# Second operations of GpSimd's minima one step later, and 97 joint minima instead of 81, in a fused top-k attention and squared-ReLU FFN kernel

## The chip, the cores and the metric

The kernel runs on one core of a Trainium2 chip. The metric is device time in microseconds (us) of one execution, taken as the median of several runs. The engines are named as in the profile: PE (TensorE, with PEld for its weight loads), DVE (VectorE), ACT (ScalarE), POOL (GpSimd) and SP (SyncE, which here only issues DMAs).

## The reference

```python
B, H, S, D = 8, 8, 576, 64; top_k = 32
scores = matmul(q, k^T) / sqrt(D)                  # per batch and head, 576 x 576
kth    = the 32nd largest of each row
attn   = softmax over the entries >= kth, 0 elsewhere
x      = (attn @ v), heads side by side            # 4608 tokens x 512
out    = relu(x @ w_in)**2 @ w_out                 # 512 -> 2048 -> 512, float32
```

## The kernel before, in words

The attention is cut into 144 **steps**, numbered u = 0 to 143 (`U = 144`). A step takes two tiles of 128 query rows (index x = 0, 1), each against all 576 keys of its head. The FFN of finished tokens is cut into pieces that are put between the steps. One Python loop writes the instructions of all engines in program order (`pin` keeps that order on each engine); each engine runs its own queue in order and waits on semaphores for the others. A main loop writes steps 0 to 124 (`Z = 125`), a second one steps 125 to 141, and the last two are written out. `DEEP = 9`: after step 11 the preparation of a step runs two steps ahead (`lead = 2`). Step 66 begins near 400 us in the profile of before, step 122 near 720 us.

For each step, the 32nd largest of 576 scores is found by DVE in four rounds of "8 largest, then remove them" (`topk`: MAX8 on L282, MATCH_REPLACE8 on L286). The rounds do not look at all 576 scores: the scores are first sorted partly, so that large ones stand in front.

- `scores(u)`: PE multiplies into the two PSUM banks sc_a and sc_b (L202); ACT copies both to `s` (L207), sc_b first.
- `split(u)`, the **pairing**: scores 0 to 287 meet scores 288 to 575. DVE takes the maxima, `tops` (L235, 128x576 for both tiles). The matching **half minima** go to `cat[288:576]`. In a "lent" step POOL makes all of them; in a step that is not lent DVE makes a quarter itself, in three operations of half the size (L237, L238, L240).
- `bring(u)`: PE copies the second half of `tops` into a part of bank sc_b (`far`, L223), so that DVE can pair it with the first half.
- `join(u)`, the **join**: DVE pairs the two halves of `tops`: maxima to `cat[0:144]` (L250), minima to `cat[144:288]` (a second L250). In a **joint** step DVE makes only the maxima, and POOL the **joint minima**.
- POOL has no minimum in use here; it computes min(a, b) as a + b - max(a, b) on the numbers' bits as integers, in two operations: an addition into its place in `cat`, and a subtraction in place. `joint_mins` does so with 128x288 (L256, L257), `small_mins` for the half minima with 128x576, or 128x288 in a step not lent (L263, L264).

Round 0 of `topk` reads `cat[0:100]`, round 1 `cat[24:144]`, round 2 `cat[0:256]` (it needs the joint minima) and round 3 all (it needs the half minima). DVE's order within step u of the main loop is: `split(u+2)`, rounds 0 to 3 of u, `join(u+2)`. POOL's order is: both operations of the joint minima of u+1, both of the half minima of u+2, squares of the FFN, the mask of u-1 (L333), now and then a cast of v (L154). SP then issues the transpose DMA of the masked weights.

Who does what is set by a planner while the program is written. `debt["G"]` and `debt["A"]` are running estimates of what POOL and ACT still owe, in us: `owe` adds, and `pass_step` takes 5.8 (POOL) and 6.0 (ACT) off at each step. By these numbers a step is lent or not (`split`), joint or not (`join`), a square of the FFN goes to ACT (L517) or POOL (L520), and a weight cast to ACT (L607) or POOL (L604).

Of the kernel before, what the change touches and what calls it, by code (L numbers as in the profile page):

```python
# [15 lines left out]
i32 = mybir.dt.int32  # L16
ALU = mybir.AluOpType
# [5 lines left out]
def kernel(  # L23
# [9 lines left out]
    nc = tc.nc  # L33
# [10 lines left out]
    HALF, QUAR = S // 2, S // 4  # L44

    def pin(ins):
        tc.keep_in_program_order(ins)
        return ins

    debt = {"G": 0.0, "A": 0.0}  # L50

    def owe(**more):
        for e, t in more.items():
            debt[e] += t
# [2 lines left out]

    def pass_step(more=0.0):
        for e in debt:
            debt[e] = max(0.0, debt[e] - {"G": 5.8, "A": 6.0}[e] - more)  # L60

    const = ctx.enter_context(tc.tile_pool(name="const", bufs=1))
    fast = ctx.enter_context(ExitStack())
# [120 lines left out]
    U = len(steps)  # L184
    Z, DEEP = U - 19, 9
# [6 lines left out]
    st = {}  # L192
# [32 lines left out]
    def split(u):  # L225
        d = st[u]
        lend = (2 < u < U - 20 and debt["G"] < 4.9) or Z < u < U - 5
        cat = d["cat"] = scp.tile([128, 2, S], f32, name="cat", bufs=3)
        tops = d["tops"] = scp.tile([128, 2, HALF], f32, name="tops", bufs=3)
        one, two = sc[0][:, :, 0:HALF], d["s"][:, :, HALF:S]  # L230
        tt = nc.vector.tensor_tensor
        if lend:
            owe(G=1.22)
            d["lent"] = True
            pin(tt(tops[:, :, :], one, two, op=ALU.max))  # L235
        else:
            pin(tt(far, one[:, :, QUAR:HALF], two[:, :, QUAR:HALF], op=ALU.max))  # L237
            pin(tt(tops[:, :, 0:QUAR], one[:, :, 0:QUAR], two[:, :, 0:QUAR], op=ALU.max))  # L238
        if not lend:
            pin(tt(cat[:, :, HALF + QUAR:S], one[:, :, QUAR:HALF], two[:, :, QUAR:HALF], op=ALU.min))  # L240
        if "rest" in d:
            d.pop("rest")()

    def join(u):
        d = st[u]
        d["joint"] = "lent" in d and DEEP + 4 <= u < U - 6 and debt["G"] < (4.5 if u < Z + 2 else 5.5)
        if d["joint"]:
            owe(G=1.6)
        for lo, op in ((0, ALU.max), (QUAR, ALU.min))[0:1 if d["joint"] else 2]:
            pin(nc.vector.tensor_tensor(d["cat"][:, :, lo:lo + QUAR], far, d["tops"][:, :, 0:QUAR], op=op))  # L250

    def joint_mins(u):
        d = st[u]
        if d["joint"]:
            at, tops = d["cat"][:, :, QUAR:HALF].bitcast(i32), d["tops"][:, :, :].bitcast(i32)
            pin(nc.gpsimd.tensor_tensor(at, tops[:, :, 0:QUAR], tops[:, :, QUAR:HALF], op=ALU.add))  # L256
            pin(nc.gpsimd.tensor_tensor(at, at, d["cat"][:, :, 0:QUAR].bitcast(i32), op=ALU.subtract))  # L257

    def small_mins(u):
        d = st[u]  # L260
        n = HALF if "lent" in d else QUAR
        s, at = d["s"], d["cat"][:, :, HALF:HALF + n].bitcast(i32)
        pin(nc.gpsimd.tensor_tensor(at, s[:, :, 0:n].bitcast(i32), s[:, :, HALF:HALF + n].bitcast(i32), op=ALU.add))  # L263
        pin(nc.gpsimd.tensor_tensor(at, at, d["tops"][:, :, 0:n].bitcast(i32), op=ALU.subtract))  # L264

    GROUP = 18
    WINDOWS = (slice(0, 100), slice(24, QUAR), slice(0, 256), slice(0, S))
# [4 lines left out]
    def topk(u, rounds=(0, 1, 2, 3), between=None):  # L272
        d = st[u]
        g = u % GROUP
        if g == 0 and 0 in rounds:
            held_m["m"] = small.tile([128, GROUP, 2, 4, 8], f32, name="m", bufs=2)
        m = d["m"] = [held_m["m"][:, g, :, r, :] for r in range(4)]
        cat = d["cat"]
        for r in rounds:
            at = WINDOWS[r]  # L280
            for x in range(2):
                pin(nc.vector.max(out=m[r][:, x, :], in_=cat[:, x, at]))  # L282
            if r == 3:
                break
            for x in range(2):
                pin(nc.vector.match_replace(out=cat[:, x, at], in_to_replace=m[r][:, x, :], in_values=cat[:, x, at], imm_value=NEG))  # L286
            if r == 1:
                negate(u)
            if r == 2 and between:
                between()  # L290
        if g == GROUP - 1 and 3 in rounds and u < U - 1:
            verify(u)
# [353 lines left out]
    scores(0)  # L646
    split(0)
    join(0)
    small_mins(0)
    scores(1)  # L650


# [20 lines left out]
    for u in range(Z):  # L673
        now[0] = u
        f = u - 4
        lead = 2 if u > DEEP + 2 else 1
        pass_step()
        owe(A=4.5 if u < DEEP + 15 else 4.12, G=3.0)
        if u > 0:
            below(u - 1, 0)  # L680
        if u == 0:
            topk(0, (0, 1))
            split(1)
            join(1)
            topk(0, (2, 3))
        elif not DEEP < u < DEEP + 3:
            split(u + lead)
        if not DEEP < u < DEEP + 3:
            ahead(u + 1 + lead)
        if u > 0:  # L690
            topk(u, (0,))
        if u == DEEP + 2:
            join(u + 1)
            split(u + 2)
            ahead(u + 3)
            bring(u + 2)
        if ok(f) and f % 2:
            invert_two(f)
        if ok(f - 1):
            place(f - 1)  # L700
        if checks:
            note()
        if lead > 1:
            joint_mins(u + 1)
        if u == DEEP + 2:
            small_mins(u + 2)
        elif u != DEEP + 1:
            small_mins(u + lead)
        dense(u, 0)
        if u and not DEEP < u < DEEP + 3:  # L710
            bring(u + lead)
        if u > 0:
            below(u - 1, 1)
            topk(u, (1,))
            if u == DEEP + 1:
                join(u + 1)
            topk(u, (2,))
            if u == DEEP + 1:
                split(u + 2)
                small_mins(u + 2)  # L720
                ahead(u + 3)
                bring(u + 2)
            topk(u, (3,))
            if u == DEEP:
                join(u + 1)
                split(u + 2)
            elif u != DEEP + 1:
                join(u + 2 if u > DEEP else u + 1)
            exps(u - 1)
            mask(u - 1)  # L730
            turn(u - 1)
        flush()
        if u == Z - 1:
            assert u % 2 == 0
            products(u - 3)
            piece()
            expo(u, 0)
            expo(u, 1)
            piece()
        else:  # L740
            dense(u, 1)
            flush()
            products(u - 3)
        if u == DEEP:
            small_mins(u + 2)
            ahead(u + 3)
            bring(u + 2)
        for _ in range(2 if u < 8 or u in (U - 22, U - 19) else 1):
            prepare(u)
        if 1 < u < 24 and not ups and not downs:  # L750
            idle_piece(2)
        turn_x(u)
        if w_casts and u >= 4:
            w_casts.pop(0)()
        if w_loads and u >= 1:
            w_loads.pop(0)()

    def weights(w):
        mask(w)
        turn(w)  # L760
# [5 lines left out]
    for u in range(Z, U - 2):  # L766
        now[0] = u
        pass_step(0.3)
        owe(A=4.12, G=3.0)
        below(u - 1, 0)  # L770
        below(u - 1, 1)
        move()
        split(u + 2)
        topk(u, (0,))
        if u == Z:
            products(u - 3)
            invert_two(u - 4)
            place(u - 5)
            place(u - 4)
        if checks:  # L780
            note()
        joint_mins(u + 1)
        small_mins(u + 2)
        if u == U - 8:
            sums_checked(nc.gpsimd, 0, OLD)
        weights(u - 1)
        square()
        hold["squares"] = False
        for go in ripe.pop(u, ()):
            go()  # L790
        ahead(u + 3)
        topk(u, (1,))
        if not piece():
            idle_piece()
        bring(u + 2)
        products(u - 2)
        topk(u, (2, 3))
        join(u + 2)
        if u == Z:
            invert(u - 3)  # L800
        invert(u - 2)
        expo(u, 0)
        expo(u, 1)
        flush()
        if u == Z:
            place(u - 3)
        place(u - 2)
        turn_x(u)
        hold["squares"] = True
        for _ in range(2 if u == U - 19 else 1):  # L810
            prepare(u)
        for n in range(3 if u >= U - 12 else 2):
            if not piece() and n == 0:
                idle_piece()
# [10 lines left out]
    u = U - 2  # L825
# [5 lines left out]
    below(u - 1, 0)  # L831
    below(u - 1, 1)
    topk(u, (0,))
    weights(u - 1)
    while downs:
        piece()
# [15 lines left out]
    for x in range(2):  # L852
        below(u, x)
        at = w[:, x, 0:S].bitcast(i32)
# [44 lines left out]
    u = U - 1  # L899
# [185 lines left out]
```

## Time and profile before

| | |
|---|---|
| median of 3 runs | 873.14 us (872.8 to 873.77) |
| the profiled execution | 873.56 us, its span 871.6 us |
| TensorE clock granted | 0.988 of full speed |
| HBM traffic | 36.70 MB read, 9.44 MB written |
| DVE's operations that the change touches | L250 x207, L235 x131, L237, L238 and L240 x13 each |
| POOL's operations that the change touches | L256 and L257 x81 each, L263 and L264 x144 each, L520 x45 |

The span is from the first to the last instruction; some 2 us lie around it. In a row of a group, "xN" is the count, then come busy us and mean ns of one, then the engine's idle time ahead of them and what ended it. In a row of the timeline come the start (us from the span's start) and the duration; "xN" merges neighbours, and a bracket tells idle time and its releaser. A row of waits reads: engine, instruction, what it waited for, total us, times, longest.

### The profile page before, as it was taken

Reading aid. Unit: us, or ns where it says so; the run is one execution under the profiler, and the core shown is the slowest. Engines: PE = TensorE matmul, PEld = TensorE weight load, DVE = VectorE, ACT = ScalarE, POOL = GpSimd, SP = SyncE. Lnnn points to the kernel's source line nnn. Section 1 sums busy time; section 2 is a strip of 40 time slices with the busy share of each in tenths; the row PEclk is TensorE's granted clock in tenths of the full one; section 3 lists DMA queues with packets and bytes.
Section 4 is the critical chain, followed back from the end, with each engine's and each line's share of the span. In section 5 each row is a group of like instructions: output and inputs, shape, how many; then the busy total and the mean of one; then the engine's idle time right before and its main releaser. Section 6 shows DMA issues by size and latency. Waiting matters only on the chain.

```text
span 871.6 us, 19893 instructions
## 1 busy us (share of the span) xinstructions
PE 755.6 (87%) x5948; PEld 482.7 (55%) x6030; DVE 842.1 (97%) x3445; ACT 809.8 (93%) x1630; POOL 787.0 (90%) x722
## 2 busy tenths in 40 slices
PE   6998997888888988889889888889888898999986
PEld 3554555555555554555555555555655564666644
DVE  5999999999999999999999999999999999999994
ACT  2888999899999998999999999999999999999973
POOL 3688999999999999999999999999999998999752
PEclk7999999999999999999999999999999999999999
DMA  5597776546565566456565455655555655424352
GB/s 122 120 223 162 178 180 106 108 97 113 92 126 108 113 112 126 80 107 115 111 115 93 101 118 108 120 120 115 121 107 116 111 101 124 85 59 86 71 85 44
DMA packets 325442, 98.04 MB, mean 112 GB/s; under 512 B 317520, under 2 KB 317776, under 8 KB 325328
## 3 DMA queue, kind: packets, MB, share of 16 engines
q1 hardware_dynamic: 323984, 96.28, 56.0%
q8 instruction: 49, 0.80, 0.4%
q10 hardware_dynamic: 1344, 0.43, 0.2%
q14 instruction: 65, 0.53, 0.2%
HBM read 36.70 MB, written 9.44 MB: 53 GB/s over the span
## 4 chain that ended last, share of the span: by engine, by line
DVE 68%; PE 12%; issue 9%; ACT 7%; POOL 3%; DMA 1%; SPq 0%; ACTq 0%; DVEq 0%; POOLq 0%
DVE m L282 28%; DVE cat L286 20%; DVE tops L235 8%; DVE cat L250 7%; PE dn_ps L534 2%; PE gen L506 2%; PE sc_b L223 2%; ACT s L207 2%; PE sc_b L202 2%; PE av_ps L404 1%; PE sc_a L202 1%; POOL cat L263 1%; ACT marks_a L328 1%; ACT h L517 1%; ACT rl L512 1%
## 5 line engine op out<-in xcount | busy, mean ns | idle before, releaser
L282 DVE MAX8 m<-cat 128x8 f32<-128x100 f32 (+3 forms) x1152 | 435.3, 419 | 0.0
L286 DVE MATCH_REPLACE8 cat<-m,cat 128x100 f32<-128x100 f32 (+2 forms) x864 | 259.4, 308 | 0.2
L264 POOL TENSOR_TENSOR cat<-cat,tops 128x576 int32<-128x576 int32 (+1 forms) x144 | 194.9, 1354 | 14.4 <-DVE tops L238 2.7
L263 POOL TENSOR_TENSOR cat<-s 128x576 int32<-128x576 int32 (+1 forms) x144 | 195.1, 1355 | 8.4 <-ACT s L207 7.4
L202 PE MATMUL sc_b<-qkT 64*128 64x288 f32 (+1 forms) x640 | 119.1, 452 | 44.6 <-DVE cat L250 34.1
L534 PE MATMUL dn_ps<-w_out,h 128*128 128x512 bf16 x492 | 133.0, 384 | 10.7 <-ACT wide L544 4.3
L506 PE MATMUL gen<-xT,w_in 128*128 128x256 bf16 (+1 forms) x1088 | 129.4, 265 | 1.1 <-ACT xT L466 0.7
L223 PE MATMUL sc_b<-tops,id_f 128*128 128x144 f32 x524 | 95.4, 305 | 39.7 <-ACT s L207 39.0
L506 PEld LDWEIGHTS <-w_in 128*128 128x128 bf16 x1344 | 110.1, 98 | 32.6 <-issue 19.5
L404 PEld LDWEIGHTS <-wT 128*128 128x128 bf16 (+3 forms) x1600 | 97.9, 99 | 48.3 <-issue 6.8
L223 PEld LDWEIGHTS sc_b<-tops,id_f 128*128 128x128 f32 x524 | 73.4, 190 | 80.4 <-ACT s L207 76.4
L328 ACT ACTIVATE marks_a<-s,m 128x576 bf16<-128x576 f32 x144 | 116.1, 811 | 0.0
L207 ACT ACTIVATE s<-sc_b 128x576 f32<-128x576 f32 x144 | 94.9, 659 | 18.1 <-PE sc_b L202 7.1
L202 PE MATMUL sc_a<-qkT 64*128 64x288 f32 (+1 forms) x640 | 110.9, 428 | 0.9 <-DVE tops L235 0.9
L328 ACT ACTIVATE marks_b<-s,m 128x576 bf16<-128x576 f32 x142 | 110.5, 784 | 0.0
L207 ACT ACTIVATE s<-sc_a 128x576 f32<-128x576 f32 x144 | 95.9, 666 | 6.5 <-PE sc_a L202 3.5
L235 DVE TENSOR_TENSOR tops<-sc_a,s 128x576 f32<-128x576 f32 x131 | 97.7, 746 | 0.0
L250 DVE TENSOR_TENSOR cat<-sc_b,tops 128x288 f32<-128x288 f32 x207 | 86.5, 443 | 4.5 <-PE sc_b L223 4.1
L202 PEld LDWEIGHTS sc_b<-qkT 64*128 64x128 f32 (+1 forms) x640 | 47.9, 177 | 73.7 <-DVE cat L250 44.3
L534 PEld LDWEIGHTS <-h 128*128 128x128 bf16 x560 | 48.0, 98 | 72.2 <-issue 34.3
L512 ACT ACTIVATE rl<-gen 128x512 f32<-128x512 f32 x140 | 84.0, 601 | 1.5 <-PE gen L506 1.5
L202 PEld LDWEIGHTS sc_a<-qkT 64*128 64x128 f32 (+1 forms) x640 | 55.3, 178 | 35.9 <-DVE tops L235 22.1
(133 smaller groups left out, 1347.7 us busy)
## 6 DMA issues: line engine op xcount, KB each, us to landing
out_dram<-wide SPq DMA_DIRECT2D x31, 256.0 KB, 2.6
q_raw<-in_q_dram SPq DMA_DIRECT2D x30, 256.0 KB, 3.7
k_raw<-in_k_dram SPq DMA_DIRECT2D x30, 256.0 KB, 3.8
h<-in_moe_w_in_dram SPq DMA_DIRECT2D x8, 512.0 KB, 5.3
h<-in_moe_w_out_dram SPq DMA_DIRECT2D x8, 512.0 KB, 4.6
v_raw_a<-in_v_dram SPq DMA_DIRECT2D x15, 256.0 KB, 4.1
v_raw_b<-in_v_dram SPq DMA_DIRECT2D x15, 256.0 KB, 3.9
out_dram<-wide SPq DMA_DIRECT2D x9, 128.0 KB, 2.4
```

The lines of the kernel that those rows point to most:

```text
L202: pin(nc.tensor.matmul(out=sc[j][r if rest else slice(0, 128), x, 0:HALF], lhsT=qkT[r, 0, c * 128:min(S, (c + 1) * 128)], rhs=qkT[r, 1, j ...
L207: pin(nc.scalar.activation(s[:, :, j * HALF:(j + 1) * HALF], sc[j][:, :, 0:HALF], AF.Copy))
L223: pin(nc.tensor.matmul(out=far[:, x, :], lhsT=id_f[:, :], rhs=st[w]["tops"][:, x, QUAR:HALF], start=True, stop=True))
L235: pin(tt(tops[:, :, :], one, two, op=ALU.max))
L250: pin(nc.vector.tensor_tensor(d["cat"][:, :, lo:lo + QUAR], far, d["tops"][:, :, 0:QUAR], op=op))
L263: pin(nc.gpsimd.tensor_tensor(at, s[:, :, 0:n].bitcast(i32), s[:, :, HALF:HALF + n].bitcast(i32), op=ALU.add))
L264: pin(nc.gpsimd.tensor_tensor(at, at, d["tops"][:, :, 0:n].bitcast(i32), op=ALU.subtract))
L282: pin(nc.vector.max(out=m[r][:, x, :], in_=cat[:, x, at]))
L286: pin(nc.vector.match_replace(out=cat[:, x, at], in_to_replace=m[r][:, x, :], in_values=cat[:, x, at], imm_value=NEG))
L328: pin(nc.scalar.activation(marks[u % 2][:, x, :], d["s"][:, x, :], AF.Relu, bias=d["m"][3][:, x, 7:8], scale=-1.0))
L506: pin(nc.tensor.matmul(out=hp[:, n * n_rows:(n + 1) * n_rows], lhsT=w_in[:, kh, (f0 + n) * 128:(f0 + n + 1) * 128], rhs=xt(kh), start=(kh ...
L534: pin(nc.tensor.matmul(out=op[:, :], lhsT=held["h2"][:, f, c * 128:(c + 1) * 128], rhs=w_out[:, f, :], start=(f == 0), stop=(f == NF - 1)))
```

## The change

1. `joint_mins` and `small_mins` become one function, `mins(u)`. It first makes the subtractions that are left over from the last call (`catch_up`), the joint one ahead of the half one; then the addition of the half minima of u, then, if the step is joint, the addition of the joint minima of u. The two subtractions wait in the list `halfway` for the next call, one step later. Up to step 11, where the preparation is not yet two steps ahead, `catch_up` is called right behind. The joint addition is so written one step earlier than before (with u+2, not with u+1).
2. Whether a step is joint is set in `split`, at the pairing, no longer in `join`. The threshold on POOL's debt is 4.9 (5.5 near the end) less 1.22, where it was 4.5 (5.5). The first step that can be joint is 14 instead of 13.
3. The planner's numbers: 5.76 us a step for POOL instead of 5.8, 2.92 owed for POOL's regular work instead of 3.0, 1.5 for a joint pair instead of 1.6.

The built program then has 97 joint pairs instead of 81, and 191 joins L250 on DVE instead of 207; 132 steps are lent instead of 131; seven squares are on ACT that were on POOL, and one weight cast on POOL that was on ACT. The subtractions of both kinds now share one line.

```diff
-            debt[e] = max(0.0, debt[e] - {"G": 5.8, "A": 6.0}[e] - more)
+            debt[e] = max(0.0, debt[e] - {"G": 5.76, "A": 6.0}[e] - more)
...
     def split(u):
         d = st[u]
         lend = (2 < u < U - 20 and debt["G"] < 4.9) or Z < u < U - 5
+        d["joint"] = lend and DEEP + 5 <= u < U - 6 and debt["G"] < (4.9 if u < Z + 2 else 5.5) - 1.22
+        if d["joint"]:
+            owe(G=1.5)
...
     def join(u):
         d = st[u]
-        d["joint"] = "lent" in d and DEEP + 4 <= u < U - 6 and debt["G"] < (4.5 if u < Z + 2 else 5.5)
-        if d["joint"]:
-            owe(G=1.6)
...
-    def joint_mins(u):
+    halfway = []
+
+    def catch_up():
+        while halfway:
+            at, top = halfway.pop(0)
+            pin(nc.gpsimd.tensor_tensor(at, at, top, op=ALU.subtract))
+
+    def mins(u):
+        catch_up()
         d = st[u]
+        cat, s, tops = [d[z][:, :, :].bitcast(i32) for z in ("cat", "s", "tops")]
+        n = HALF if "lent" in d else QUAR
+        at = cat[:, :, HALF:HALF + n]
+        pin(nc.gpsimd.tensor_tensor(at, s[:, :, 0:n], s[:, :, HALF:HALF + n], op=ALU.add))
+        halfway.append((at, tops[:, :, 0:n]))
         if d["joint"]:
-            at, tops = d["cat"][:, :, QUAR:HALF].bitcast(i32), d["tops"][:, :, :].bitcast(i32)
+            at = cat[:, :, QUAR:HALF]
             pin(nc.gpsimd.tensor_tensor(at, tops[:, :, 0:QUAR], tops[:, :, QUAR:HALF], op=ALU.add))
-            pin(nc.gpsimd.tensor_tensor(at, at, d["cat"][:, :, 0:QUAR].bitcast(i32), op=ALU.subtract))
-
-    def small_mins(u):
-        d = st[u]
-        n = HALF if "lent" in d else QUAR
-        s, at = d["s"], d["cat"][:, :, HALF:HALF + n].bitcast(i32)
-        pin(nc.gpsimd.tensor_tensor(at, s[:, :, 0:n].bitcast(i32), s[:, :, HALF:HALF + n].bitcast(i32), op=ALU.add))
-        pin(nc.gpsimd.tensor_tensor(at, at, d["tops"][:, :, 0:n].bitcast(i32), op=ALU.subtract))
+            halfway.insert(0, (at, cat[:, :, 0:QUAR]))
...
-        owe(A=4.5 if u < DEEP + 15 else 4.12, G=3.0)
+        owe(A=4.5 if u < DEEP + 15 else 4.12, G=2.92)
...
-        if lead > 1:
-            joint_mins(u + 1)
         if u == DEEP + 2:
-            small_mins(u + 2)
+            mins(u + 2)
         elif u != DEEP + 1:
-            small_mins(u + lead)
+            mins(u + lead)
+        if u < DEEP + 3:
+            catch_up()
...
     for u in range(Z, U - 2):
...
-        joint_mins(u + 1)
-        small_mins(u + 2)
+        mins(u + 2)
```

More of the change, by code (lines that the diff above doesn't have):

```diff
@@ L648 @@
     join(0)
-    small_mins(0)
+    mins(0)
+    catch_up()
     scores(1)
@@ L702 @@
             note()
-        if lead > 1:
-            joint_mins(u + 1)
         if u == DEEP + 2:
-            small_mins(u + 2)
+            mins(u + 2)
         elif u != DEEP + 1:
-            small_mins(u + lead)
+            mins(u + lead)
+        if u < DEEP + 3:
+            catch_up()
         dense(u, 0)
@@ L719 @@
                 split(u + 2)
-                small_mins(u + 2)
+                mins(u + 2)
+                catch_up()
                 ahead(u + 3)
@@ L744 @@
         if u == DEEP:
-            small_mins(u + 2)
+            mins(u + 2)
+            catch_up()
             ahead(u + 3)
@@ L768 @@
         pass_step(0.3)
-        owe(A=4.12, G=3.0)
+        owe(A=4.12, G=2.92)
         below(u - 1, 0)
@@ L781 @@
             note()
-        joint_mins(u + 1)
-        small_mins(u + 2)
+        mins(u + 2)
         if u == U - 8:
@@ L833 @@
     topk(u, (0,))
+    catch_up()
     weights(u - 1)
```

## The prediction

> **What bounds the kernel now.** I read the page first, then the busy time by stage, then what each engine waits for in those stages.
>
> ```profile
> PE 755.6 (87%) x5948; PEld 482.7 (55%) x6030; DVE 842.1 (97%) x3445; ACT 809.8 (93%) x1630; POOL 787.0 (90%) x722
> ```
>
> Three engines are over 89% here, so shares of the whole span decide nothing. The table by stage (columns: stretch, its length, then busy us and instruction counts of PE, PEld, DVE, ACT, POOL) says more:
>
> ```profile
> 100.00:400.00 300.00, 258.25 (x2008) 164.66 (x2032) 299.48 (x1233) 290.40 (x581) 291.35 (x261) 0.99 0.58 114
> 400.00:700.00 300.00, 261.80 (x2104) 171.00 (x2132) 299.77 (x1232) 297.62 (x605) 291.68 (x260) 1.00 0.59 113
> 700.00:820.00 120.00, 110.88 (x911) 72.30 (x922) 115.53 (x483) 116.41 (x243) 111.45 (x101) 0.99 0.43 86
> ```
>
> From 100 to 700 us DVE is never idle (599.25 of 600): it sets the pace. ACT has 9.6 us free in the first half and 2.4 in the second, POOL about 8.5 in each. What each waited for in those windows, DVE for 100 to 700, then ACT for 100 to 400 (its two largest), then ACT for 400 to 700 (all):
>
> ```profile
> DVE cat L250 <- PE sc_b L223: 0.2, 1, 0.2
> ```
> ```profile
> ACT s L207 <- DVE cat L286: 3.9, 3, 1.5
> ACT s L207 <- DVE m L282: 3.1, 5, 1.3
> ```
> ```profile
> ACT s L207 <- PE sc_a L202: 0.5, 2, 0.3
> ACT qkT L138 <- PE gen L134: 0.4, 2, 0.2
> ACT s L207 <- ACT marks_a L328: 0.3, 1, 0.3
> ```
>
> DVE waits 0.2 us in 600. ACT waits at least 7.0 us in the first 300, and there it waits for DVE: it would follow a faster DVE. In the second 300 it waits 1.2 us: it has almost nothing left. So time taken off DVE is time off the kernel until ACT, the next engine, is late. POOL's idle time must be looked into, because the change loads it.
>
> POOL's timeline (start, duration):
>
> ```profile
> 532.16 1.41 POOL L263 TENSOR_TENSOR cat<-s 128x576 int32<-128x576 int32 x1
> 533.65 1.41 POOL L264 TENSOR_TENSOR cat<-cat,tops 128x576 int32<-128x576 int32 x1
> 535.02 1.41 POOL L333 TENSOR_TENSOR w_two_b<-w_two_b,marks_a 128x576 int32<-128x576 int32 x1
> ...
> 537.88 0.80 POOL L256 TENSOR_TENSOR cat<-tops 128x288 int32<-128x288 int32 x1
> 538.75 0.80 POOL L257 TENSOR_TENSOR cat<-cat 128x288 int32<-128x288 int32 x1
> 539.51 1.41 POOL L263 TENSOR_TENSOR cat<-s 128x576 int32<-128x576 int32 x1
> 540.99 1.40 POOL L264 TENSOR_TENSOR cat<-cat,tops 128x576 int32<-128x576 int32 x1
> ```
>
> The subtraction L264 starts 1.49 us after its addition L263 and the mask L333 only 1.37 after L264, though all last 1.41; in the joint pair L257 starts 0.87 after L256, and L263 0.76 after L257. An instruction that reads what the one ahead of it wrote starts some 0.08 us after that one's end; one that does not starts 0.04 us before it. POOL's idle time is this: about 0.12 us a pair, not slack. POOL waits for nobody here; it is simply late behind DVE.
>
> **The change, part by part.** The built program's order gives the counts: joint pairs on POOL 81 to 97, DVE's second join operation (L250) 207 to 191, lent steps 131 to 132; seven squares move from POOL to ACT (in steps 33, 46, 49, 50, 61, 105 and 133 of 0 to 143; step 66 begins near 400 us, step 122 near 720), one weight cast from ACT to POOL (step 11).
>
> *DVE.* Two joins in a row, and the pairing that follows; then, one step on, a pairing and the round that follows:
>
> ```profile
> 538.13 0.81 DVE L250 TENSOR_TENSOR cat<-sc_b,tops 128x288 f32<-128x288 f32 x2
> 538.85 0.75 DVE L235 TENSOR_TENSOR tops<-sc_a,s 128x576 f32<-128x576 f32 x1
> ```
> ```profile
> 544.49 0.74 DVE L235 TENSOR_TENSOR tops<-sc_a,s 128x576 f32<-128x576 f32 x1
> 545.15 0.41 DVE L282 MAX8 m<-cat 128x8 f32<-128x100 f32 x2
> ```
>
> From the first join to the pairing are 0.72 us, so a join that goes is worth 0.36: 16 x 0.36 = 5.8. The added lent step replaces three operations of the join's size (about 3 x 0.36 = 1.08) by one of 0.66 (544.49 to 545.15): 0.4 more. DVE: -6.2 us in all. [...]
>
> *POOL.* The 16 new joint pairs cost two operations at the independent spacing, 2 x 0.76 = 1.5: 24 us. A subtraction one step later no longer follows its own addition. That holds for all 81 old joint pairs and for 130 of 144 half pairs (for the first 14, catch_up stands right behind): 211 x 0.12 = 25 us less. The squares:
>
> ```profile
> L520 POOL TENSOR_TENSOR h<-rl 128x512 bf16<-128x512 f32 x45 | 46.5, 1042 | 1.1 <-ACT rl L512 1.1
> ```
>
> Seven at about 1.0 go: -7. The cast is about +1 (the square's size, 1.04), the added lent step 2 x (1.37 - 0.76) = +1.2. Sum 24 - 25 - 7 + 1 + 1.2 = -6 us: POOL carries the new work with what it no longer loses, and drops as much as DVE.
>
> *The later subtraction.* Does DVE now wait for it? DVE needs the joint minimum's subtraction before the first replace of round 0 (which overwrites what it reads) and the half minimum's before round 3:
>
> ```profile
> 539.95 0.25 DVE L286 MATCH_REPLACE8 cat<-m,cat 128x100 f32<-128x100 f32 x1
> ```
> ```profile
> 542.80 1.41 DVE L282 MAX8 m<-cat 128x8 f32<-128x576 f32 x2
> ```
>
> This is the tightest place of the steady part: L257 ended at 539.55, 0.40 us ahead of the replace. In the new order the joint subtraction stands first in POOL's step, in L256's place: 537.88 + 0.76 = 538.64, 1.3 ahead. The half subtraction follows, to 540.0; round 3 starts at 542.80, 2.8 us later. So the move costs nothing while POOL is no more than 1.3 us later than today, and its sum says it is not. The instructions queued behind it on POOL in that step (half addition, joint addition, mask) are the same number as before, so mask and the transpose DMA behind it on SP do not move; SP and its order are untouched. At the step's head the joint subtraction could wait for DVE's join, but the join is at 538.85 for the following step, and the one it needs lies a whole step earlier.
>
> *ACT.* Seven squares more:
>
> ```profile
> L517 ACT ACTIVATE h<-rl 128x512 bf16<-128x512 f32 x95 | 60.8, 640 | 0.0
> ```
> ```profile
> 673.23 0.65 ACT L207 ACTIVATE s<-sc_b 128x576 f32<-128x576 f32 x1
> 673.76 0.66 ACT L207 ACTIVATE s<-sc_a 128x576 f32<-128x576 f32 x1
> ...
> 673.93 0.76 PE L223 MATMUL sc_b<-tops,id_f 128*128 128x144 f32 x4 [1.38 <-ACT s L207]
> ...
> 674.80 0.46 DVE L250 TENSOR_TENSOR cat<-sc_b,tops 128x288 f32<-128x288 f32 x1 [0.21 <-PE sc_b L223]
> ```
>
> Queued ACT rows overlap (0.53 from a 0.65 us copy to the next), so a square costs about 0.52, at most 0.64: +3.6 us, at most 4.5. The rows also show what a late ACT does: its copy of sc_b ends at 673.88, PE's matmuls L223 start 0.05 later and end at 674.69, and the join waits for them. Early in the kernel the same chain has room:
>
> ```profile
> 206.20 0.72 PE L223 MATMUL sc_b<-tops,id_f 128*128 128x144 f32 x4
> ...
> 208.94 0.44 DVE L250 TENSOR_TENSOR cat<-sc_b,tops 128x288 f32<-128x288 f32 x1
> ```
>
> There 2.0 us lie between L223's end and the join. So ACT is what comes late next, and only past about 600 us.
>
> *The cast.* It leaves ACT just ahead of a late join:
>
> ```profile
> 91.68 0.76 PE L223 MATMUL sc_b<-tops,id_f 128*128 128x144 f32 x4 [0.26 <-ACT s L207]
> ...
> 92.55 0.46 DVE L250 TENSOR_TENSOR cat<-sc_b,tops 128x288 f32<-128x288 f32 x1 [1.28 <-PE sc_b L223]
> ```
>
> DVE lost 1.28 there, but L223 waited only 0.26 for ACT: -0.3, not the whole cast.
>
> **The sum, by stage.** By 400 us seven net joins and the added lent step go: 7 x 0.36 + 0.4 = 2.9. ACT must follow and do five squares (2.6), together 5.5 against at least 7.0 of its waits: paid in full, -2.9. From 400 to 720 seven more joins: 2.5 wanted. ACT has 1.2 of waits and one square more (0.5): it can surely give 0.7, all 2.5 if the room between copy and join that is left at 400 us carries it. I take -1.1, nearer the sure end, since the rows at 674 show that room already used up. From 720 on two joins (0.7) and one square; ACT is busy 116.4 of 120 there and DVE not the only bound: 0, between -0.7 and +0.5. With the cast: -0.3 - 2.9 - 1.1 = -4.3 us. The profiled execution took 873.56 (span 871.6 and 2.0 around it), 0.42 over the median of 873.14; I take the difference off the median: 868.8. Its own bounds: -0.3 - 2.9 - 2.5 - 0.7 = -6.4 (866.7) and -0.3 - 2.9 - 0.7 + 0.5 = -3.4 (869.7).
>
> **Rivals.** (1) *ACT takes it back.* If a square costs its whole 0.64 and ACT cannot use its waits, 4.5 of the 6.2 + 0.3 return: -2.0, 871.1. If nothing is gained past 400 us and five squares at 0.64 (3.2) eat the 0.3 + 2.9 of the first part, there is no change: 873.1. For it: 297.62 of 300 busy. Against it: in the first half ACT waits for DVE itself, and only two of the seven squares fall past 400 us. I put this case at 872.0.
>
> (2) *POOL becomes the bound: slower.* The place is round 3 (and the first replace) waiting for POOL; the price is the new work if the 0.12 does not come back, because it belongs to each second operation and not to its place behind the first. Then POOL has 24 - 7 + 1 + 1.2 = +19 us; 1.3 us are covered by the lateness allowed above, the rest is DVE waiting: +18, 891. It decides from the point where the move saves less than 18/211 = 0.085 of the 0.12 us a pair. [...]
>
> (3) *DVE's gain in full:* -6.4, 866.7, if ACT's room suffices to the end.
>
> That the change does not do what it says is excluded by the order: 97 joint pairs, their subtractions at the next step's head.
>
> **Chances.** Forecast 0.55, (3) 0.17, (1) 0.14, (2) 0.14. About 0.2%, 1.75 us, is what a measurement of this kernel can tell from no change. Faster: 0.55 + 0.17 = 0.72; same: 0.14; slower: 0.14. The range runs from (3) to the far end of (1), 866.7 to 873.1, and leaves out (2).
>
> **What would show it.** Right: L250 x191 with DVE still idle-free from 100 to 600 us; the gap ahead of subtractions gone, 0.76 and 1.37 between starts; ACT's waits for DVE smaller; more of DVE L250 waiting for PE L223 past 600 us, but under 2 us. Wrong: DVE L282 or L286 waiting for POOL (case 2), or L250 waiting for L223 for several us from 400 us on (case 1).

## The result and the profile after

The changed kernel takes 870.89 us (median of 21 runs, 869.58 to 874.03), the kernel before 873.0 us (21 runs beside them, 871.89 to 874.58). The ratio is 0.9977, 95% interval 0.9970 to 0.9983: 2.1 us faster, where 4.3 were forecast. The profiled execution took 870.89 us, its span 868.9.

The page's first line and the table by stage, as they were shown of before:

```profile
PE 759.9 (87%) x6034; PEld 483.6 (56%) x6034; DVE 837.5 (96%) x3427; ACT 811.2 (93%) x1636; POOL 797.9 (92%) x748
...
100.00:400.00 300.00, 261.81 (x2059) 166.12 (x2057) 299.49 (x1232) 294.25 (x590) 297.70 (x274) 1.00 0.58 116
400.00:700.00 300.00, 261.03 (x2112) 170.12 (x2110) 297.65 (x1224) 297.90 (x607) 296.62 (x272) 1.00 0.56 111
```

From 100 to 400 us DVE is as full as before (299.49 of 300), and POOL is now full too: the gaps ahead of its subtractions have become work. From 400 to 700 us DVE has lost 2.1 us of busy time against before (299.77), and ACT has gained almost nothing (297.62 to 297.90): DVE is no longer alone in setting the pace. What DVE waits for in 400 to 700 us, then what ACT waits for in the same stretch (all its rows):

```profile
DVE cat L250 <- PE sc_b L223: 1.5, 5, 0.3
DVE cat L292 <- issue: 0.3, 1, 0.3
DVE shares L421 <- PE av_ps L410: 0.2, 1, 0.2
```
```profile
ACT s L207 <- PE sc_a L202: 0.7, 3, 0.3
ACT qkT L138 <- PE gen L134: 0.4, 2, 0.2
```

The joins' wait for L223, 0.2 us in one place before, is 1.5 us in five. (L292 is the replace, L282's MAX8 is now L288, both subtractions are L257, the half addition is L265, the joint addition L269, the mask L339, ACT's square L523.) One of the five, in the timeline:

```profile
622.22 0.77 ACT L334 ACTIVATE marks_b<-s,m 128x576 bf16<-128x576 f32 x1
...
622.89 0.62 ACT L523 ACTIVATE h<-rl 128x512 bf16<-128x512 f32 x1
...
623.41 0.64 ACT L207 ACTIVATE s<-sc_b 128x576 f32<-128x576 f32 x1
...
624.10 0.76 PE L223 MATMUL sc_b<-tops,id_f 128*128 128x144 f32 x4 [0.24 <-ACT s L207]
...
624.96 0.46 DVE L250 TENSOR_TENSOR cat<-sc_b,tops 128x288 f32<-128x288 f32 x1 [0.32 <-PE sc_b L223]
```

ACT is queued without a gap: mark, square, copy of sc_b. The copy ends at 624.05, PE starts 0.05 later, and the join comes 0.32 us late. The square holds ACT for 0.52 us (622.89 to 623.41), more than the join's 0.32. In the version between the two, below, that square is on POOL: there the copy follows right behind the mark (622.09), and the join (623.81) waits for nothing.

POOL's spacing, at about the place of the timeline shown of before:

```profile
534.03 0.80 POOL L257 TENSOR_TENSOR cat<-cat 128x288 int32<-128x288 int32 x1
534.78 1.41 POOL L257 TENSOR_TENSOR cat<-cat,tops 128x576 int32<-128x576 int32 x1
536.14 1.41 POOL L265 TENSOR_TENSOR cat<-s 128x576 int32<-128x576 int32 x1
537.50 0.80 POOL L269 TENSOR_TENSOR cat<-tops 128x288 int32<-128x288 int32 x1
538.26 1.41 POOL L339 TENSOR_TENSOR w_two_c<-w_two_c,marks_b 128x576 int32<-128x576 int32 x1
```

Starts are 0.75 or 0.76 us apart behind a small operation and 1.36 behind a large one, subtractions included. The 0.12 us a pair came back as forecast.

**Where the time went, step by step.** The first MAX8 of each step's round 0 gives 144 marks that both traces share. Between them stand these differences, after minus before, with DVE's busy and idle time from the starts and ends of all its instructions:

| steps | length before | change | DVE busy | DVE idle | forecast |
|---|---|---|---|---|---|
| up to 11 | 79.77 us | -0.84 | | | none |
| 11 to 14 | 19.45 | -0.58 | +0.31 | -0.89 | +0.1 (the cast -0.3, step 13's join +0.36) |
| 14 to 68 | 309.90 | -3.02 | -2.99 | -0.01 | -3.3 (eight joins, the lent step) |
| 68 to 122 | 307.97 | **+0.70** | -1.32 | +2.02 | **-1.1** |
| 122 to 143 | 130.33 | -0.50 | -0.62 | +0.12 | 0 |
| behind the start of 143 | 24.13 | **+1.62** | | | none |

Step 68 begins at 409 us in the trace of before, step 122 at 717. The prediction's seven net joins by 400 us, -2.9 with the lent step, are eight that go between steps 14 and 68 and one, step 13's, that comes back on DVE ahead of them; its own prices are put to the rows so. From step 11 to 68 the kernel became 3.6 us shorter, where 3.2 were forecast; up to step 122 it then became 0.7 us longer, where 1.1 more were to be gained; and the last 25 us, which the prediction did not touch, gave 1.6 back.

### The profile page after: what moved, and what is told of

The parts are those of the page before. It is cut to its first block, busy times and chain, and to the rows that moved or that the text cites. A ratio compares the mean times of both kernels' runs of the same rounds, so it can differ in the third digit from the quotient of the medians.

```text
span 868.9 us, 20007 instructions
## 1 busy us (share of the span) xinstructions
PE 759.9 (87%) x6034; PEld 483.6 (56%) x6034; DVE 837.5 (96%) x3427; ACT 811.2 (93%) x1636; POOL 797.9 (92%) x748
## 4 chain that ended last, share of the span: by engine, by line
DVE 54%; POOL 18%; issue 13%; PE 10%; ACT 4%; DMA 1%; SPq 0%; POOLq 0%; DVEq 0%; ACTq 0%
DVE m L288 24%; DVE cat L292 15%; POOL cat L257 7%; DVE tops L238 7%; DVE cat L250 6%; POOL cat L265 5%; POOL cat L269 2%; PE sc_b L223 1%; PE dn_ps L540 1%; ACT s L207 1%; PE sc_b L202 1%; POOL w_two_b L339 1%; PE gen L512 1%; PE dn_ps L562 1%; PE av_ps L410 1%
## 5 line engine op out<-in xcount | busy, mean ns | idle before, releaser
L288 DVE MAX8 m<-cat 128x8 f32<-128x100 f32 (+3 forms) x1152 | 435.3, 419 | 0.1
L292 DVE MATCH_REPLACE8 cat<-m,cat 128x100 f32<-128x100 f32 (+2 forms) x864 | 259.3, 308 | 0.3 <-issue 0.3
L265 POOL TENSOR_TENSOR cat<-s 128x576 int32<-128x576 int32 (+1 forms) x144 | 196.8, 1366 | 6.7 <-ACT s L207 6.5
L257 POOL TENSOR_TENSOR cat<-cat,tops 128x576 int32<-128x576 int32 (+1 forms) x144 | 196.6, 1365 | 1.9 <-DVE tops L238 0.8
L540 PE MATMUL dn_ps<-w_out,h 128*128 128x512 bf16 x560 | 145.7, 385 | 4.4 <-ACT wide L550 4.4
L202 PE MATMUL sc_b<-qkT 64*128 64x288 f32 (+1 forms) x640 | 118.4, 447 | 32.4 <-DVE cat L250 23.2
L223 PE MATMUL sc_b<-tops,id_f 128*128 128x144 f32 x528 | 96.6, 306 | 51.5 <-ACT s L207 51.0
L223 PEld LDWEIGHTS sc_b<-tops,id_f 128*128 128x128 f32 x528 | 73.4, 189 | 94.8 <-ACT s L207 91.3
L202 PE MATMUL sc_a<-qkT 64*128 64x288 f32 (+1 forms) x640 | 109.0, 420 | 0.9 <-DVE tops L238 0.9
L250 DVE TENSOR_TENSOR cat<-sc_b,tops 128x288 f32<-128x288 f32 x191 | 80.8, 443 | 4.2 <-PE sc_b L223 3.8
L202 PEld LDWEIGHTS sc_b<-qkT 64*128 64x128 f32 (+1 forms) x640 | 48.1, 175 | 59.8 <-DVE cat L250 31.6
L269 POOL TENSOR_TENSOR cat<-tops 128x288 int32<-128x288 int32 x97 | 78.3, 807 | 0.0
```

Source lines behind the costliest of these rows:

```text
L202: pin(nc.tensor.matmul(out=sc[j][r if rest else slice(0, 128), x, 0:HALF], lhsT=qkT[r, 0, c * 128:min(S, (c + 1) * 128)], rhs=qkT[r, 1, j ...
L223: pin(nc.tensor.matmul(out=far[:, x, :], lhsT=id_f[:, :], rhs=st[w]["tops"][:, x, QUAR:HALF], start=True, stop=True))
L257: pin(nc.gpsimd.tensor_tensor(at, at, top, op=ALU.subtract))
L265: pin(nc.gpsimd.tensor_tensor(at, s[:, :, 0:n], s[:, :, HALF:HALF + n], op=ALU.add))
L540: pin(nc.tensor.matmul(out=op[:, :], lhsT=held["h2"][:, f, c * 128:(c + 1) * 128], rhs=w_out[:, f, :], start=(f == 0), stop=(f == NF - 1)))
```

## The experiments

Two theories for the missing half. **ACT**: past 400 us ACT's copy, not DVE, sets the join, so that each further square on ACT costs its time. **POOL**: the later subtractions and 16 more pairs make the first replace or round 3 wait. A third, **the clock**, came up from the traces' tails.

**The parts of the change by themselves.** In these kernels the choices that the planner makes are written out as lists. The first has the new order with the choices of before (lent steps, squares and casts as before, 80 joint pairs, because step 13 can't be one in the new order); the second the old order with all choices of after (97 joint pairs, the squares, the cast and the lent step; there `joint` is still set in `join`); the third is the changed kernel with the seven squares back on POOL.

```diff
-        lend = (2 < u < U - 20 and debt["G"] < 4.9) or Z < u < U - 5
-        d["joint"] = ...
+        lend = u in LENT
+        d["joint"] = u in JOINT
...
-                    if DEEP + 15 < now[0] < U - 7 and debt["A"] < 5.4 and debt["G"] > 5.0:
+                    if next(SQUARES) == "A":
...
-                    if debt["A"] > debt["G"]:
+                    if next(CASTS) == "G":
```

*The new order alone.* 

> The new order of POOL's operations with the old decisions: the lent steps, squares and casts of before and its joint steps (80: step 13, whose join comes too late for the new order, is left out). DVE's work is that of before plus one join, 0.36 us; ACT's is that of before; POOL loses about 25 us of waits. ACT theory and forecast: DVE sets the pace as before, so -0.5 to +0.5 us. POOL theory (POOL's lateness costs time already in before): faster by more than 1 us.

Measured: 873.12 us beside 873.2, ratio 0.9995 (0.9981 to 1.0009). Its steps lie within 0.4 us of those of before, but for steps 104 to 114, which begin 0.7 us later; by step 143 0.2 of that is left. The rows by stage:

```profile
100.00:400.00 300.00, 258.37 (x2008) 164.77 (x2032) 299.49 (x1233) 290.39 (x581) 288.67 (x262) 0.99 0.57 115
400.00:700.00 300.00, 263.04 (x2103) 170.62 (x2131) 299.62 (x1231) 297.54 (x606) 288.71 (x259) 1.00 0.58 112
```

The move by itself costs nothing and brings nothing: DVE is as full as before, and POOL now waits for others with what it saved.

*The joint pairs alone.* 

> The old order, each subtraction right behind its addition, with all decisions of the changed kernel (97 joint steps, its squares and casts). POOL carries 24 us of joint pairs and sheds 7 us of squares, without the 25 us that the order saves. Forecast: POOL falls behind by 15 to 20 us, DVE L292 waits for it, and the kernel is 10 to 18 us slower than before. If POOL has room, as a rival has it: the same 2 us faster as the changed kernel.

Measured: 888.38 us, ratio 1.0175 (1.0155 to 1.0195): 15.2 us slower. DVE's longest wait from 100 to 820 us, and one case of it (L261 is the joint subtraction there, L260 its addition):

```profile
DVE cat L290 <- POOL cat L261: 15.7, 26, 1.7
```
```profile
498.61 0.80 POOL L260 TENSOR_TENSOR cat<-tops 128x288 int32<-128x288 int32 x1
499.49 0.80 POOL L261 TENSOR_TENSOR cat<-cat 128x288 int32<-128x288 int32 x1
```
```profile
500.32 0.09 DVE L290 MATCH_VALUE_LOAD cat<-m,cat 128x8 f32 x1 [0.96 <-POOL cat L261]
```

This is rival (2) of the prediction brought about on purpose: where the 0.12 us a pair is not saved, DVE waits for the new work on POOL. It was priced at 18. So the order alone is worth nothing, the pairs without it cost 15 us, and both together save 2.

*The squares back on POOL.* 

> The changed kernel with the squares of before: the seven that went to ACT are POOL's again, joints, lent steps and casts unchanged. ACT theory: ACT has 3.6 us less, the waits of L250 for L223 between 400 and 700 us shrink, and the time is 1 to 2 us below the changed kernel's. POOL theory: POOL has 7 us more, its last free time; DVE waits for it in round 0 and the time is 2 to 6 us above the changed kernel's.

Measured: 872.09 us, ratio 0.9985 (0.9970 to 0.9999), 1.2 us behind the changed kernel measured beside it (below), with intervals that overlap. ACT's theory had it 1 to 2 us below the changed kernel, POOL's 2 to 6 above, and neither range was met. The steps tell why: from 68 to 122 it does gain (-0.34 against before, where the changed kernel has +0.70), and DVE's waits of L250 for L223 between 400 and 700 us shrink from 1.5 us in five places to 0.5 in two, as ACT's theory has it. But from 50 to 56 it is 1.76 us longer than before (the changed kernel: 0.40, of which 0.29 is a pause of DVE at 303.3 us behind operations of POOL that had long ended). Three squares stand close together there (steps 46, 49 and 50), POOL is late, and the first replace waits, for the subtraction (L261 here):

```profile
DVE cat L296 <- POOL cat L261: 1.7, 3, 0.9
```
```profile
335.00 0.09 DVE L296 MATCH_VALUE_LOAD cat<-m,cat 128x8 f32 x1 [0.89 <-POOL cat L261]
```

Both theories hold, each in its place: POOL has no room for these squares ahead of step 56, ACT none for those behind step 60.

**Is it ACT past 400 us?** In 31 steps ACT's second mark is made half as wide for one of the two tiles, in the changed kernel and in the kernel before; its other half is left as an earlier step made it.

```diff
-        pin(nc.scalar.activation(marks[u % 2][:, x, :], d["s"][:, x, :], AF.Relu, ...))
+        n = HALF if x == 1 and u % 2 == 0 and 60 <= u < 121 else S
+        pin(nc.scalar.activation(marks[u % 2][:, x, 0:n], d["s"][:, x, 0:n], AF.Relu, ...))
```

*In the changed kernel.* 

> The changed kernel with ACT relieved: in the 31 even steps from 60 to 120 the second mask operation covers 288 columns instead of 576 and the rest of that mask is left from an earlier step, so some weights are masked wrongly. ACT has 0.25 to 0.4 us less in each, 8 to 12 us in all. ACT theory (between steps 66 and 122 ACT, through its copy and PE's L223, holds DVE's join up): DVE's waits of L250 there go, and the kernel is 1.5 to 2.5 us below the changed kernel's 870.9. POOL theory (POOL without gaps, no waits left): no change from 870.9.

*In the kernel before.* 

> The same relief of ACT in the kernel before, masks equally wrong. DVE waits 0.2 us in 100 to 700 us there, so all theories: -0.2 to -0.8 us against before.

Measured: 867.93 us beside 872.9, ratio 0.9945 (0.9933 to 0.9957), for the changed kernel; 873.2, ratio 1.0000 (0.9990 to 1.0011), for the kernel before. From 400 to 700 us, the changed kernel's row, DVE's only wait in it, and the row of the kernel before with the same relief:

```profile
400.00:700.00 300.00, 266.74 (x2147) 171.43 (x2146) 299.56 (x1234) 295.45 (x613) 299.00 (x274) 1.00 0.59 113
```
```profile
DVE cat L292 <- issue: 0.3, 1, 0.3
```
```profile
400.00:700.00 300.00, 267.57 (x2136) 170.39 (x2135) 300.00 (x1235) 294.21 (x609) 292.60 (x261) 1.00 0.60 114
```

The joins' wait for L223 is gone and DVE is full again. From step 68 to 122 the changed kernel becomes 3.2 us shorter, the kernel before 0.7. So ACT is what held the changed kernel there, and hardly held the kernel before. DVE's idle time shows only part of it (2.02 us): a join that comes up to some 0.08 us late only loses its overlap with the instruction ahead of it (in the trace of before the join at 544.13 us starts 0.08 us ahead of that one's end), and DVE's busy time falls by another 1.15 us with the same work once ACT is relieved; 0.8 of overlap comes back at the joins alone. The whole times missed what was expected on both sides: the changed kernel gained 2.96 us instead of 1.5 to 2.5, and the kernel before nothing in its median instead of 0.2 to 0.8. In the trace of the latter the steps up to 140 had gained 1.6, and 1.0 of it was lost behind, beside a stretch of half clock at 834.5 us (below).

**A version between the two.** Squares of steps 33, 46, 49 and 50 on ACT as in the changed kernel, those of 61, 105 and 133 on POOL as before (lists written out as above).

> The changed kernel with the squares of steps 33, 46, 49 and 50 on ACT as it has them, and from step 61 on all squares as before (61, 105 and 133 on POOL again). ACT theory: the first part gains as in the changed kernel, 3.6 us by step 66; past it ACT has 1.0 us less and the loss of 0.7 us between steps 68 and 122 turns into a gain of 0.3: 0.5 to 1.0 us below the changed kernel, the best of all so far. POOL theory: POOL has 2 us more, the time is up to 1 us above the changed kernel's.

Measured: 869.86 us beside 872.9, ratio 0.9965 (0.9952 to 0.9978). Steps 68 to 122 are now 0.58 us shorter than before instead of 0.70 longer: two squares less on ACT by then (61 and 105) are worth 1.28 us. At step 104, ahead of the second one, the gain over the changed kernel is 0.64; it is nearly twice that at step 122. So each is worth about its whole duration, and not the 0.52 us between the starts of queued ACT rows; why it is the whole, the traces don't show. It has the lowest median of the kernels that compute everything; its interval overlaps that of the changed kernel, so only the gain against the kernel before is shown, and the one between those steps.

**The clock.** The changed kernel run again beside the first three:

> The changed kernel itself once more, for its time beside the three below on the same chip and for a second trace. All theories: 0.9977 of before, about -2.0 us. ACT theory (ACT, with seven more squares, is the bound from step 66 on): again DVE waits of 1 to 2 us between 400 and 700 us, all of L250 for L223, and again no gain between steps 68 and 122. Clock theory (what was lost in the tail is PE's clock, which fell to half there by chance): the half-clock stretches lie at other places, and the time from step 143 to the end is shorter than 25.7 us unless one of them falls there again.

Measured: 870.88 us (868.89 to 873.49), ratio 0.9975 (0.9961 to 0.9988). Its trace agrees with the first one to 0.15 us up to step 143 and is then 1.9 us shorter. The half-clock stretches do not lie at other places, as the clock theory had it: they begin at 13.2 and 832.4 us, in the first trace at 13.3 and 832.5, and only the first trace's third, at 849.5, is not there. The same stretch of the tail in the first trace, then in the second; the last three columns of a row are granted clock, DMA share and GB/s:

```profile
850.00:855.00 5.00, 5.00 (x51) 3.77 (x50) 2.04 (x5) 0.88 (x3) 0.00 (x0) 0.70 0.02 3
```
```profile
850.00:855.00 5.00, 4.95 (x63) 3.69 (x62) 2.57 (x7) 1.67 (x5) 0.79 (x3) 1.00 0.01 3
```
```profile
851.57 1.72 PE L540 MATMUL dn_ps<-w_out,h 128*128 128x512 bf16 x4
```
```profile
850.55 1.03 PE L540 MATMUL dn_ps<-w_out,h 128*128 128x512 bf16 x4
```

In the first trace PE ran at half clock (0.50 granted) from 849.5 to 852.9 us, on matmuls that the end waits for: four took 1.72 instead of 1.03 us. In the trace of before that stretch of the tail has the full clock (1.00 granted from 852 to 860 us). In the 3.41 us ahead of the first trace's stretches at 832.5 and 849.5 us PE was busy 0.52 and 1.96 us; from 146.4 us on it was busy only 1.92 of 3.41 us, too, and the granted clock stayed at 1.00. So it is not shown that idle PE brings a stretch on. In case it does, PE was kept busier ahead of it, with six matmuls of zeros:

```diff
+    def keep_warm(n):
+        for j in range(n):
+            pin(nc.tensor.matmul(out=one[:, j % 2, :], lhsT=zero[:, :], rhs=fill[:, :], start=False, stop=False))
...
+    keep_warm(3)
...
+    keep_warm(3)
```

> The changed kernel with six matmuls of zeros more in the last 25 us, put where PE idles (three ahead of the last-but-one products, three ahead of the first matmuls of the last FFN block), adding zeros to a bank. Clock theory (the median of the changed kernel contains runs in which PE's clock falls to half near the end, because a window of 3.4 us with idle PE came just ahead): 0.7 to 1.5 us below the changed kernel's median and a narrower spread. If the clock is not behind it: no change, or up to 0.3 us slower.

Measured: 872.12 us (869.55 to 874.38), ratio 0.9984 (0.9972 to 0.9995): no gain, and a spread no smaller. In its trace the tail behind step 143 is as short as the shortest (23.8 us), but a half-clock stretch twice as long stands just ahead, at 836 to 843 us, and the start-up is 2.9 us longer than in the changed kernel's first trace. So a remedy is not shown. Nor is it shown that the matmuls made that stretch longer: the two kernels with ACT relieved, which lack them, have one of the same length there (at 830.6 and 834.5 us).

Whether the steady part or only the ends vary from run to run was asked with two more traces of each kernel.

> The kernel before once more, for a second trace. The profiled execution of the changed kernel is 2.67 us shorter than that of the kernel before, and a second trace of the changed kernel 4.67 us; the medians differ by 2.1. Theory A (the clock's phase): from the start of step 1 to the start of step 143 the kernel before takes the same time in each trace, within 0.4 us, and traces differ only ahead of step 1 and behind step 143, where PE's half-clock stretches fall differently; the changed kernel is then 3.1 to 3.9 us shorter between those steps in every pair of traces. Theory B (the steady part itself varies): the time between steps 1 and 143 differs by over 1 us from the first trace.

> The kernel before, a third trace. Theory A: steps 1 to 143 within 0.4 us of the first trace. Theory B: over 1 us off.

> The changed kernel, a third trace. Theory A: between the starts of steps 1 and 143 within 0.4 us of the first two traces, which agree to 0.07; the part behind step 143 1 to 2 us longer where a half-clock stretch falls on PE's last pieces of the FFN, as in the first trace, and not in the second. Theory B: over 1 us off between steps 1 and 143.

> The changed kernel, a fourth trace. As for the third: theory A within 0.4 us between steps 1 and 143, theory B over 1 us off.

| traces | start of step 1 | steps 1 to 143 | step 143 to DVE's last instruction | from there to the end |
|---|---|---|---|---|
| before, three | 20.12, 19.79, 19.30 us | 827.31, 827.31, 827.44 | 18.98, 18.99, 18.99 | 5.14, 4.83, 5.27 |
| changed, four | 19.34, 19.35, 19.05, 19.27 | 823.85, 823.78, 824.18, 823.74 | 20.64, 18.99, 19.81, 20.64 | 5.11, 4.83, 5.72, 5.09 |

Theory A holds: between steps 1 and 143 each kernel repeats itself to 0.45 us (three of the four changed traces to 0.12; in the third a half-clock stretch falls at 73 us), and the changed kernel is 3.1 to 3.7 us shorter there in every pairing. Some 0.8 of that belongs to the clock too: all three traces of before have a stretch at 741 us and no changed one has it. From step 126 to 128, where it falls, the changed kernel gains 0.84 us; the version between the two, which has a stretch at 736.8 us in the same step, gains 0.07. Behind step 143 both kernels need 18.98 or 18.99 us when no half-clock stretch falls there: the work is the same. In the changed kernel it was 1.65 longer twice, with a stretch at 849.5 and at 849.3 us, and 0.83 once, with one at 841.3. The last output's way to the end adds up to 0.9 more, for which the traces show no cause. By the middle traces the difference is -0.5 ahead of step 1, where the change alters nothing, -3.5 between and +1.5 behind, -2.5 in all, beside -2.1 in the medians.

The traces also tell when the stretch at 849.5 us comes. Within each trace all half-clock stretches begin on one grid of 3.413 us (in the first changed trace 832.483 and 849.549 lie 240 and 245 such steps behind 13.284). In all thirteen traces without the matmuls of zeros, count from the start of step 143 to the grid's line between 4 and 7 us behind it. In three it lies at 6.11 (squares back on POOL), 6.32 and 6.36 us (the changed kernel's fourth and first), and a stretch begins there. In the other ten it lies at 4.2 to 4.9 us or from 6.38 us on (6.38 in the changed kernel's second trace, 6.45 to 6.52 in the three of before), and none does. So the place of the work on that grid goes with the 1.65 us, and the changed kernel stands right at the edge; that 0.02 us decide is read from these traces alone.

## Why the prediction was half right

The time was missed: of 4.3 us, 2.1 came.

**DVE's gain, and the first half of the sum: right.** Steps 14 to 68 became 3.02 us shorter, where eight joins and the lent step were priced at 3.3, and all of it is DVE's busy time. A removed join was worth about its spacing, 0.36 us, not its full duration: at 0.45 us each (the 0.81 of two joins less 0.36), the same eight joins and the lent step's 0.4 would have brought 4.0. The cast brought 0.54 instead of 0.3: with step 13's join added, the stage from step 11 to 14 became 0.58 shorter, and only 0.04 in the new order alone, which lacks the cast's move.

**POOL: right.** The spacing came back at each subtraction, its busy time rose to 797.9 us without becoming the bound, and the later subtraction cost nothing by itself. Rival (2) needed the gap to stay, and with it the 15 us came (18 were priced). But POOL's room was nearly used up, as the seven squares showed when they came back.

**The term that was mis-sized: "From 400 to 720 seven more joins: 2.5 wanted ... I take -1.1".** Measured +0.7. The demand was right: with ACT relieved the stretch is 2.5 us shorter than before (1.8 against the kernel before with the same relief). The step that failed is what ACT was said to be able to give. It was wrong even at its "sure" end, 0.7. That end came from 1.2 us of ACT's waits less one square. But the rows of those waits put 0.9 of the 1.2 down to PE (sc_a L202, gen L134), not to DVE. Those two did not shrink as DVE's work did: 0.7 and 0.4 us of them are there after. (The third, 0.3 us, is put down to a mark of ACT's that had ended 0.34 us before; a replace of DVE's ended 0.08 us ahead of that copy, at 540.20 us.) That the named releaser is the reason fits these rows, but no experiment takes it by itself; that ACT had nothing to give, the relief shows. Only in the first half did ACT wait mainly for DVE, and there its waits for DVE fell from 7.0 to 2.3 us. What was left over after the first half was no reserve either: at step 66 the room between L223's end and the join's start had fallen from 1.17 to 0.36 us. The square of step 61 alone took 0.55 of that (0.91 in the version between, which has it on POOL); at step 61 itself the room was still that of before (1.50 and 1.46). From there the squares of steps 61 and 105 cost the kernel about their whole 0.64 us each. So past 400 us rival (1) took over, for that stage alone. Its sign was L250 waiting for L223 "for several us": the rows show 1.5 us in five places, and some 0.8 more are lost overlap. By the prediction's own list, under 2 us past 600 us, this would have passed for right: the signs did not tell the two cases apart. That the whole, -2.1, nearly meets that rival's first price, -2.0, is chance: the price had the squares cost time in every stage, and nothing of what the ends gave back.

**From 720 us on**: 0 forecast, -0.5 measured, within the bounds given, but by luck: the half-clock stretch at 741 us in the traces of before accounts for it. The version between the two, with a stretch at the same place, is 0.35 us slower than before from step 122 to 143.

**What the sum left out: the ends.** The sum ran from step 11 to 143, where -4.3 was forecast and -3.4 measured, some 0.8 of it by the stretch just named; it took the rest of the span as unchanged. The last work returned 0.8 to 1.7 us in three of four traces, and the clock is its cause: without a half-clock stretch it takes the same 18.99 us as before. In which trace the stretch of 1.65 us comes goes with the place of step 143 on the clock's grid, as told above: 6.32 to 6.38 us for three changed traces, at the edge, and 6.45 to 6.52 for before, beyond it. The sum could not have known this from the one trace it had.

## What to carry to other kernels

When the bound engine gets work taken away, look up for each wait of the next engine who releases it: here ACT's waits for the bound engine could be turned into gain (7.0 us fell to 2.3), and those for a third one stayed (0.9 us before, 1.1 after). Work moved between two nearly full helpers belongs where each still has room, and that differs by stage: here POOL had none just ahead of step 56 and ACT none behind step 60. Two edits can each be worthless or harmful alone and pay together, so try the pair before judging a part.

## What the hardware showed besides

The half-clock stretches of PE in these traces (0.50 granted) come in multiples of 3.4 us (3.4 and 6.8, and 10.2 or 13.7 at the start-up of some runs; the last one of a trace is cut off by its end). Behind the start-up they come back at the same places of a kernel: at 140, 741 and 836 us in all three traces of before, within 0.7 us, and at 832 in three of the four changed ones. Only the changed kernel's third trace, whose grid lies 1.2 to 1.4 us off that of the other changed ones, has them elsewhere (73, 138, 326 and 841 us). Two traces of one kernel were 2.0 us apart, 1.65 of it by one such stretch. Within each trace the stretches lie on a grid of 3.413 us, and it lies differently in each trace. The 2.0 us are 0.23% of the kernel's time. That is also the size of this change, so a single pair of traces could have shown -2.6 or -4.6 us.

In these traces an extra wait goes with a small price even if it is long satisfied. The operation behind the last MAX8 of round 0 starts 0.164 us after that one's start in steps that aren't joint, and 0.184 to 0.186 in joint ones, where it waits for POOL's subtraction besides, in all seven traces of the two kernels (medians over steps 27 to 117). In the changed kernel's first trace that subtraction had by then ended 1.8 us earlier (median over the same steps).
